# Mixture-of-experts kernel: the second products of a group pair in two groups of three, and another order of the seven first products

## The chip, the cores and the metric

The kernel runs on one core of one Trainium2 chip. The metric is the device time of one execution in microseconds, the median of several runs.

## What is computed

Three layers follow each other: attention with a global and a local part, a mixture of experts whose gate is made even by eight Sinkhorn rounds, and a gated linear layer. The change lies in the second one:

```python
def _moe_ref(x, w_gate, w1, w2):
    N, D = x.shape                      # 1536, 512
    E = w_gate.shape[1]                 # 8
    ...
    for e in range(E):
        h = np.maximum(x @ w1[e], 0.0)  # w1[e]: 512 x 1024
        ye = h @ w2[e]                  # w2[e]: 1024 x 512
        out += P[:, e:e + 1] * ye
    return out.astype(np.float32)
```

All values are float32. The kernel keeps each operand of a matmul as a high part (float32r) and a low part, the remainder, and makes a product from three matmuls: high x high, high x low, low x high (`product`, lines 362 to 370). The lines 368, 369 and 370 are these three, wherever the product comes from.

## The kernel before

Expert 0 is done first, in plain products, while attention and the gate are being computed. Experts 1 to 7 follow in 28 *visits*, seven experts by four quarters of w1's columns (256 columns and the matching 256 rows of w2). Each visit is done by `run_fast` and consists of two *pairs*, one for each half of the batch; a pair is two groups of 384 tokens. There are thus 56 pairs. After them the gated layer runs.

In a pair (`pair`, from line 506) the hidden values x w1 of both token groups, for 2 x 128 columns, are computed with seven block products instead of eight, from sums of blocks of w1 and sums of blocks of x. The seven are the calls `run(0, ...)` to `run(6, ...)`, here R0 to R6. Each is six matmuls with 384 columns of tokens. Three of them read sums of x's blocks, which were formed once and stand in `th` and `tl`; four read blocks of x itself, in `xh` and `xl`. The w1 side is one of seven *forms*, high and low, which `form_step` makes for the next visit: ACT rounds (line 201), POOL takes the remainder (line 202).

The seven results are put together in three PSUM banks x, y and z. A run with `start=False` adds to what stands in its bank. Before it may do so, the earlier content has to be taken: by ACT's copy into `snap` (`copied`, line 560), or by DVE's sum of the bank and a copy (`summed`, line 556), which is followed by ACT's rectified high part (`hidden`, line 546) and DVE's low part (line 548). The low part is put off: it is queued in `late` and issued by `rest()`.

Second products belong to the pair before: six units stand in `pending`, three with the hidden values t, three with o. A unit (`unit_second`), here S, is six matmuls with 512 columns of w2 into one of four banks. Then DVE multiplies the bank by the gate and adds it to the accumulator (line 451); this is called the take-off below. `seconds(count)` issues that many units, and after each one it issues all that is in `late` and calls `slots(None)`.

The order is written out by hand, and each engine works through its own queue in that order:

```python
run(0, x, block(0, 0)); copied(0, x); slots(0)
run(1, z, trans(0)); copied(1, z); slots(1)
seconds(1)
run(2, x, trans(1), start=False); copied(2, x); slots(2)
seconds(1)
run(3, z, block(1, 1), start=False); summed(t_hid, 0, z, snap[:, 2]); slots(3)
seconds(1)
run(4, x, trans(2), start=False); summed(t_hid, 1, x, snap[:, 1]); slots(4)
seconds(1)
run(5, y, block(1, 0)); summed(o_hid, 0, y, snap[:, 0]); slots(5)
seconds(2)
run(6, x, block(0, 1), start=False); hidden(o_hid, 1, x); slots(6)
```

`slots` is called 13 times a pair, seven times after a run and six times after an S. Each call is a *tick*. In the first pair of a visit the ticks after an S issue POOL's four additions of w1's blocks for the next visit (`sum_steps`, line 273). In the second pair the ticks after a run issue the next visit's forms, from the one after R1 on, and the first two ticks after an S issue the splits of the two halves of w2 (128 x 512 each). The seventh form follows the second pair.

Every tick also drives `doubles`. The gated layer's weights come as doubles, and are turned into float32 in 36 pieces in the `work` tile, spread over the ticks of the first 26 visits: 12 steps a piece, 440 steps with eight empty ones over 676 ticks. Six of the twelve issue an operation on DVE (lines 315, 322, 328, 335, 340, 345); the first of these is a shift that ACT converts (line 318) in the same step, two also end in one on POOL (348, 351), one loads and one stores.

Of the kernel before, what the change touches and what calls it, by code (L numbers as in the profile page):

```python
# [66 lines left out]
def tile_global_local_attention__then__sinkhorn_moe__then__glu(  # L67
# [132 lines left out]
    def split_one(r, h, lo):  # L200
        nc.scalar.activation(out=h, in_=r, func=AF.Copy)  # L201
        nc.gpsimd.tensor_tensor(out=lo, in0=r, in1=h.bitcast(F32), op=ALU.subtract)  # L202
# [47 lines left out]
    def form(i):  # L250
        a, col = (1, i) if i < 4 else (0, i - 4)
        cols = slice(col * FQ, (col + 1) * FQ)
        return wh[a][0][:, cols], wl[a][0][:, cols]

    def w1_blocks(n):
        r = raw[visits[n]["raw"]][:, 0 : 4 * FQ]
        r = r.rearrange("p (k f c) -> p f k c", k=KD, f=2)
        return {(i, j): r[:, i, 2 * j : 2 * j + 2, :] for i in range(2) for j in range(2)}

    def tall(ap):  # L260
        return ap.rearrange("p (k c) -> p k c", k=2)

    def sums():
        return [tall(state["sums"][:, i * FQ : (i + 1) * FQ]) for i in range(4)]
# [11 lines left out]

    def form_step(n, i):
        a, (s1, s2, s3, s4) = w1_blocks(n), sums()
        src = (a[0, 0], s1, s2, s4, s3, a[0, 1], a[1, 1])[i]
        h, lo = form(i)  # L280
        split_one(src, tall(h), tall(lo))

# [79 lines left out]
    def product(ps, pairs, start=True):  # L362

        n = len(pairs)
        for i, (ah, al, bh, bl) in enumerate(pairs):
            first, end = start and i == 0, i == n - 1
            mm = dict(out=ps, skip_group_check=not start)
            nc.tensor.matmul(lhsT=ah, rhs=bh, start=first, stop=False, **mm)  # L368
            nc.tensor.matmul(lhsT=ah, rhs=bl, start=False, stop=False, **mm)  # L369
            nc.tensor.matmul(lhsT=al, rhs=bh, start=False, stop=end, **mm)  # L370
# [22 lines left out]
    def next_hid():  # L393
        state["hid"] += 1
        return (state["hid"] - 1) % HID
# [38 lines left out]
    def unit_second(n, t, at, j):  # L434
        vis = visits[n]
        ps = state["Y"].next()
        second(vis, hid[at], j, ps)
        a = acc(t)
        if vis["kind"] != "glu":
            if vis.get("start"):  # L440
                nc.vector.tensor_copy(out=a, in_=ps)
            elif vis["e"] == 0:
                nc.vector.tensor_tensor(out=a, in0=ps, in1=a, op=ALU.add)
            else:
                gate = state["gate"]
                e = vis["e"]
                if e == 1 and vis["f"] == 0:
                    nc.vector.tensor_scalar(
                        out=a, in0=a, scalar1=gate[:, t, 0:1], scalar2=None, op0=ALU.mult
                    )  # L450
                nc.vector.scalar_tensor_tensor(  # L451
                    out=a, in0=ps, scalar=gate[:, t, e : e + 1], in1=a,
                    op0=ALU.mult, op1=ALU.add,
                )
        elif vis["f"] == 0:
            nc.vector.tensor_copy(out=a, in_=ps)
        elif vis["f"] < NFF - 1:
            nc.vector.tensor_tensor(out=a, in0=ps, in1=a, op=ALU.add)
        else:
            o = state["o"].next()  # L460
            nc.vector.tensor_tensor(out=o, in0=ps, in1=a, op=ALU.add)
            nc.sync.dma_start(out=out[t * P : (t + 1) * P, :], in_=o)
# [38 lines left out]
    def tokens(k, s, b, half):  # L501

        at = b * S + half * C
        return xh[:, 2 * k + s, at : at + C], xl[:, 2 * k + s, at : at + C]

    def pair(n, b, slots):


        th, tl = state["t"]
        snap, pre = state["snap"], state["pre"]  # L510
        x, y, z = state["X"].next()[:, :C], state["P2"][:, :C], state["P5"][:, :C]
        t_hid, late = next_hid(), []
        pending, done = state["pending"], []

        def run(i, ps, rhs, start=True):
            h, lo = form(i)
            product(
                ps,
                [
                    (h[:, s * P : (s + 1) * P], lo[:, s * P : (s + 1) * P], *rhs(s))  # L520
                    for s in range(2)
                ],
                start,
            )

        def trans(i):
            return lambda s: (th[:, i, s, b, :], tl[:, i, s, b, :])

        def block(k, half):
            return lambda s: tokens(k, s, b, half)  # L530

        def rest():
            for step in late:
                step()
            late.clear()

        def seconds(count):
            for _ in range(count):
                if pending:
                    unit_second(*pending.pop(0))  # L540
                rest()
                slots(None)

        def hidden(at, f, src):
            hh, hl = hid[at]
            nc.scalar.activation(out=hh[:, f, :C], in_=src, func=AF.Relu)  # L546
            late.append(
                lambda: nc.vector.scalar_tensor_tensor(  # L548
                    out=hl[:, f, :C], in0=src, scalar=0.0, in1=hh[:, f, :C].bitcast(F32),
                    op0=ALU.max, op1=ALU.subtract,  # L550
                )
            )

        def summed(at, f, ps, kept):
            p = pre.next()
            nc.vector.tensor_tensor(out=p, in0=ps, in1=kept, op=ALU.add)  # L556
            hidden(at, f, p)

        def copied(i, ps):
            nc.scalar.activation(out=snap[:, i], in_=ps, func=AF.Copy)  # L560

        run(0, x, block(0, 0))
        copied(0, x)
        slots(0)
        run(1, z, trans(0))
        copied(1, z)
        slots(1)
        seconds(1)
        run(2, x, trans(1), start=False)
        copied(2, x)  # L570
        slots(2)
        seconds(1)
        run(3, z, block(1, 1), start=False)
        summed(t_hid, 0, z, snap[:, 2])
        slots(3)
        seconds(1)
        run(4, x, trans(2), start=False)
        summed(t_hid, 1, x, snap[:, 1])
        slots(4)
        seconds(1)  # L580
        run(5, y, block(1, 0))
        o_hid = next_hid()
        summed(o_hid, 0, y, snap[:, 0])
        slots(5)
        seconds(2)
        run(6, x, block(0, 1), start=False)
        hidden(o_hid, 1, x)
        slots(6)
        for unit in pending:
            unit_second(*unit)  # L590
        rest()
        base = b * TB
        state["pending"] = [(n, base + TC + j, t_hid, j) for j in range(TC)]
        state["pending"] += [(n, base + j, o_hid, j) for j in range(TC)]
# [496 lines left out]
    late = ctx.enter_context(tc.tile_pool(name="late", bufs=1))  # L1091
# [27 lines left out]
    def trans_steps(b):  # L1119


        r21, r11, r12, r22 = (
            work[:, i * 2 * C : (i + 1) * 2 * C].rearrange("p (s c) -> p s c", s=2)
            for i in range(4)
        )

        def block(k, half):
            at = b * S + half * C
            part = slice(2 * k, 2 * k + 2), slice(at, at + C)
            return xh[:, part[0], part[1]], xl[:, part[0], part[1]]  # L1130

        def whole(out, k, half):
            h, lo = block(k, half)
            return lambda: nc.gpsimd.tensor_tensor(
                out=out, in0=h.bitcast(F32), in1=lo.bitcast(F32), op=ALU.add
            )

        def less(out, x, y):
            return lambda: nc.vector.tensor_tensor(out=out, in0=x, in1=y, op=ALU.subtract)

        def put(r, h, lo):
            return lambda: split_one(r, h, lo)

        return [
            whole(r11, 0, 0), whole(r12, 0, 1), whole(r22, 1, 1), whole(r21, 1, 0),
            less(r11, r12, r11), put(r11, th[:, 0, :, b, :], tl[:, 0, :, b, :]),
            less(r12, r22, r12), put(r12, th[:, 2, :, b, :], tl[:, 2, :, b, :]),
            less(r22, r22, r11), put(r22, th[:, 1, :, b, :], tl[:, 1, :, b, :]),
            less(r21, r21, r22), put(r21, *block(0, 1)),
        ]  # L1150
# [94 lines left out]
    trans = [trans_steps(b) for b in range(B)]  # L1245
    side = Paced(gate_steps(), 5 * (NB0 - NA) + 5 * CB * NQ - 4)
    rest = NB0 - NA - 1
# [118 lines left out]
```

## Time and profile before

| | |
|---|---|
| median of 3 runs | 1448.43 us (1444.64 to 1449.32) |
| profiled execution, time | 1444.89 us |
| profiled execution, span of its instructions | 1442.4 us |
| PE busy | 1424.5 us, 99% |
| DVE / ACT / POOL busy | 862.6 / 505.3 / 567.9 us |
| chain that ended last | PE 95%, DVE 2%, ACT 1%, POOL 1%, issue 1% |
| first and last matmul on `th` | 259.2 and 1123.4 us |

The profile lists TensorE twice: PE is the matmuls, PEld the weight loads, which run beside the matmul before. A busy PE only means that a matmul was under way; the pace is read from the distance between the starts of two matmuls. A wait before a matmul sits on its weight load.

### The profile page before, as it was taken

To read this page: it belongs to the slowest core of one execution; us is meant where nothing else is said; L and a number is where in the kernel's file an instruction comes from. 1 tells how busy PE (TensorE), PEld (TensorE's weight loads), DVE (VectorE), ACT (ScalarE), POOL (GpSimd) and SP (SyncE) were. 2 spreads that over 40 slices of the span, in tenths; PEclk is the share of its full clock that TensorE was granted. 3 is DMA by queue.
4 is the path that set the end of the run, shared out by engine and by line. 5 is a ranking of instruction groups with operands and counts; after the bars stand their busy time and mean duration, and the time that the engine had idled before them with its cause. 6 is when DMAs were issued, how large, how long until landed. Compare 5 with 4: busy or idle time off the path is not lost.

```text
span 1442.4 us, 19809 instructions
## 1 busy us (share of the span) xinstructions
PE 1424.5 (99%) x7286; PEld 1229.5 (85%) x7287; DVE 862.6 (60%) x1655; ACT 505.3 (35%) x1152; POOL 567.9 (39%) x618
## 2 busy tenths in 40 slices
PE   8999999999999999999999999999999999999998
PEld 4666888999999999899899999999989888888887
DVE  6676476676657666666676676766665543333333
ACT  5777222433333333333333333333333321222111
POOL 4554454554354453444444444445442221112110
PEclk9999999999999999999999999999999999999999
DMA  7751011132121222221213212212210110010002
GB/s 180 165 141 45 16 45 59 45 103 73 52 74 52 73 73 82 73 69 57 73 52 102 74 52 74 74 52 80 82 51 30 44 45 15 30 44 30 0 1 88
DMA packets 99192, 92.60 MB, mean 64 GB/s; under 512 B 55312, under 2 KB 73744, under 8 KB 99088
## 3 DMA queue, kind: packets, MB, share of 16 engines
q1 hardware_dynamic: 98800, 91.26, 20.4%
q8 instruction: 59, 0.97, 0.3%
q14 instruction: 45, 0.37, 0.1%
q10 hardware_dynamic: 288, 0.00, 0.0%
HBM read 78.66 MB, written 12.58 MB: 63 GB/s over the span
## 4 chain that ended last, share of the span: by engine, by line
PE 95%; DVE 2%; ACT 1%; POOL 1%; issue 1%; DMA 0%; DVEq 0%; ACTq 0%; SPq 0%; POOLq 0%
PE bank L368 30%; PE bank L370 30%; PE bank L369 30%; PE bank L867 1%; PE bank L919 1%; PE bank L905 1%; PE bank L841 1%; ACT e L881 0%; DVE e L875 0%; POOL wl L202 0%; PE bank L1314 0%; POOL e L893 0%; DMA lens<-in_n_local_dram 0%; DMA qr<-in_q_dram 0%; DVE kT L845 0%
## 5 line engine op out<-in xcount | busy, mean ns | idle before, releaser
L451 DVE SCALAR_TENSOR_TENSOR acc<-bank,gate,acc 128x512 f32<-128x512 f32 x336 | 251.7, 749 | 233.8 <-PE bank L370 231.5
L370 PE MATMUL bank<-wh,hl 128*128 128x512 f32 x912 | 358.6, 393 | 0.0
L202 POOL TENSOR_TENSOR wl<-raw,wh 128x512 fp32r<-128x512 f32 (+1 forms) x196 | 209.6, 1086 | 377.4 <-ACT wh L201 377.3
L368 PE MATMUL bank<-wh,hh 128*128 128x512 f32 x912 | 358.1, 393 | 0.0
L369 PE MATMUL bank<-wl,hh 128*128 128x512 f32 x912 | 356.9, 391 | 0.0
L368 PE MATMUL bank<-xh,wh 128*128 128x384 f32 (+1 forms) x720 | 252.8, 351 | 1.1 <-ACT aT L906 1.1
L370 PE MATMUL bank<-xh,wl 128*128 128x384 f32 (+1 forms) x720 | 251.0, 349 | 0.0
L369 PE MATMUL bank<-xl,wh 128*128 128x384 f32 (+1 forms) x720 | 250.0, 347 | 0.0
L370 PEld LDWEIGHTS bank<-wh,hl 128*128 128x128 f32 x912 | 171.0, 188 | 37.6
L546 ACT ACTIVATE hh<-kept 128x384 fp32r<-128x384 f32 x168 | 88.1, 525 | 312.1 <-DVE kept L556 312.1
L368 PEld LDWEIGHTS bank<-wh,hh 128*128 128x128 f32 x912 | 171.4, 188 | 27.1 <-issue 1.3
L369 PEld LDWEIGHTS bank<-wl,hh 128*128 128x128 f32 x912 | 171.3, 188 | 26.2
L368 PEld LDWEIGHTS bank<-xh,wh 128*128 128x128 f32 x720 | 135.2, 188 | 15.0 <-ACT aT L906 1.3
L369 PEld LDWEIGHTS bank<-xl,wh 128*128 128x128 f32 x720 | 135.2, 188 | 13.5 <-DVE xl L1319 0.5
L370 PEld LDWEIGHTS bank<-xh,wl 128*128 128x128 f32 x720 | 135.0, 188 | 5.7
L202 POOL TENSOR_TENSOR wl<-work,wh 128x256 fp32r<-128x256 f32 x112 | 93.8, 839 | 99.4 <-ACT wh L201 96.4
L560 ACT ACTIVATE kept<-bank 128x384 f32<-128x384 f32 x168 | 82.4, 491 | 120.0 <-PE bank L370 119.9
L548 DVE SCALAR_TENSOR_TENSOR hl<-kept,hh 128x384 fp32r<-128x384 f32 x168 | 112.4, 669 | 1.3 <-ACT hh L546 1.3
L370 PE MATMUL bank<-th,wl 128*128 128x384 f32 x336 | 113.0, 336 | 0.0
L368 PE MATMUL bank<-th,wh 128*128 128x384 f32 x336 | 112.4, 334 | 0.0
L369 PE MATMUL bank<-tl,wh 128*128 128x384 f32 x336 | 112.4, 334 | 0.0
L426 DVE TENSOR_TENSOR z<-bank,sg 128x512 f32<-128x512 f32 x36 | 24.9, 692 | 136.2 <-PE bank L370 136.2
(143 smaller groups left out, 1855.3 us busy)
## 6 DMA issues: line engine op xcount, KB each, us to landing
raw<-in_moe_w_dram SPq DMA_DIRECT2D x72, 512.0 KB, 4.3
glw<-work SPq DMA_DIRECT2D x36, 256.0 KB, 2.3
raw<-glw SPq DMA_DIRECT2D x18, 512.0 KB, 3.2
work<-in_moe_w_gate_dram SPq DMA_DIRECT2D x12, 512.0 KB, 3.9
work<-in_moe_w_val_dram SPq DMA_DIRECT2D x12, 512.0 KB, 4.0
work<-in_moe_w_out_dram SPq DMA_DIRECT2D x12, 512.0 KB, 3.9
qr<-in_q_dram SPq DMA_DIRECT2D x32, 96.0 KB, 2.7
kr<-in_k_dram SPq DMA_DIRECT2D x32, 96.0 KB, 2.8
```

The source lines that it names most:

```text
L202: nc.gpsimd.tensor_tensor(out=lo, in0=r, in1=h.bitcast(F32), op=ALU.subtract)
L368: nc.tensor.matmul(lhsT=ah, rhs=bh, start=first, stop=False, **mm)
L369: nc.tensor.matmul(lhsT=ah, rhs=bl, start=False, stop=False, **mm)
L370: nc.tensor.matmul(lhsT=al, rhs=bh, start=False, stop=end, **mm)
L426: nc.vector.tensor_tensor(out=z, in0=ps, in1=sg, op=ALU.mult)
L451: nc.vector.scalar_tensor_tensor(out=a, in0=ps, scalar=gate[:, t, e : e + 1], in1=a, op0=ALU.mult, op1=ALU.add,)
L546: nc.scalar.activation(out=hh[:, f, :C], in_=src, func=AF.Relu)
L548: lambda: nc.vector.scalar_tensor_tensor(out=hl[:, f, :C], in0=src, scalar=0.0, in1=hh[:, f, :C].bitcast(F32), op0=ALU.max, op1=ALU.subtract,)
L560: nc.scalar.activation(out=snap[:, i], in_=ps, func=AF.Copy)
L841: nc.tensor.transpose(ps[:, j * P : (j + 1) * P], raw_[u % QKB][:, j, :], ident)
L867: nc.tensor.matmul(out=ps[j][:, lo:KW], lhsT=qT[rows, own], rhs=kT[rows, keys], start=True, stop=True,)
L905: nc.tensor.transpose(ps[:, j, a, :], e[:, j, a * P : (a + 1) * P], ident)
```

## The change

R0 and R1 change places, and so do R2 and R3, each with its bank, and with them the forms 0 and 1, and 2 and 3. The second products stand in two groups of three: after R3 and after R6, instead of singly after R1, R2, R3 and R4 and in two after R5. The first product behind each group (R4, and R0 of the next pair) reads a sum of x's blocks. `rest` can issue a number of the put-off low parts, and one is issued behind R5 and one behind R6, ahead of the tick.

```diff
--- before.py
+++ after.py
@@ -276,7 +276,7 @@
 
     def form_step(n, i):
         a, (s1, s2, s3, s4) = w1_blocks(n), sums()
-        src = (a[0, 0], s1, s2, s4, s3, a[0, 1], a[1, 1])[i]
+        src = (s1, a[0, 0], s4, s2, s3, a[0, 1], a[1, 1])[i]
         h, lo = form(i)
         split_one(src, tall(h), tall(lo))
 
@@ -529,10 +531,10 @@
         def block(k, half):
             return lambda s: tokens(k, s, b, half)
 
-        def rest():
-            for step in late:
+        def rest(count=None):
+            for step in late[:count]:
                 step()
-            late.clear()
+            del late[:count]
 
         def seconds(count):
             for _ in range(count):
@@ -559,33 +561,32 @@
         def copied(i, ps):
             nc.scalar.activation(out=snap[:, i], in_=ps, func=AF.Copy)
 
-        run(0, x, block(0, 0))
+        run(0, z, trans(0))
+        copied(1, z)
+        slots(0)
+        run(1, x, block(0, 0))
         copied(0, x)
-        slots(0)
-        run(1, z, trans(0))
-        copied(1, z)
         slots(1)
-        seconds(1)
-        run(2, x, trans(1), start=False)
+        run(2, z, block(1, 1), start=False)
+        slots(2)
+        run(3, x, trans(1), start=False)
         copied(2, x)
-        slots(2)
-        seconds(1)
-        run(3, z, block(1, 1), start=False)
         summed(t_hid, 0, z, snap[:, 2])
         slots(3)
-        seconds(1)
+        seconds(3)
         run(4, x, trans(2), start=False)
         summed(t_hid, 1, x, snap[:, 1])
         slots(4)
-        seconds(1)
         run(5, y, block(1, 0))
         o_hid = next_hid()
         summed(o_hid, 0, y, snap[:, 0])
+        rest(1)
         slots(5)
-        seconds(2)
         run(6, x, block(0, 1), start=False)
         hidden(o_hid, 1, x)
+        rest(1)
         slots(6)
+        seconds(3)
         for unit in pending:
             unit_second(*unit)
         rest()
```

The line numbers of the changed kernel are higher by one up to two: `summed` is at 558, `copied` at 562, `hidden` at 548 and 550. Two places of the order, by engine, follow.

DVE in the second pair of a visit, from the first take-off of a second product issued behind R3 to the sums of R4 (`kept<-bank_64`) and R5. `acc<-bank` is a take-off, `hl<-kept,hh` a low part, `work<-work` a step of the doubling. Before:

```order
L451 SCALAR_TENSOR_TENSOR acc_75<-bank_68,gate,acc_75 128x512
L548 SCALAR_TENSOR_TENSOR hl_77<-kept,hh_76 128x384
L328 SCALAR_TENSOR_TENSOR work<-work 128x512
L556 TENSOR_TENSOR kept<-bank_64,kept 128x384
L451 SCALAR_TENSOR_TENSOR acc_75<-bank_69,gate,acc_75 128x512
L548 SCALAR_TENSOR_TENSOR hl_77<-kept,hh_76 128x384
L335 TENSOR_SCALAR work<-work 128x512
L556 TENSOR_TENSOR kept<-bank_65,kept 128x384
```

In the changed kernel:

```order
L451 SCALAR_TENSOR_TENSOR acc_75<-bank_70,gate,acc_75 128x512
L550 SCALAR_TENSOR_TENSOR hl_77<-kept,hh_76 128x384
L451 SCALAR_TENSOR_TENSOR acc_75<-bank_67,gate,acc_75 128x512
L322 TENSOR_SCALAR work<-work 128x512
L451 SCALAR_TENSOR_TENSOR acc_75<-bank_68,gate,acc_75 128x512
L328 SCALAR_TENSOR_TENSOR work<-work 128x512
L558 TENSOR_TENSOR kept<-bank_64,kept 128x384
L558 TENSOR_TENSOR kept<-bank_65,kept 128x384
```

R4's sum stood behind one take-off, one low part and one step of the doubling; now three take-offs, one low part and two steps stand ahead of it, the last step directly ahead. The sum behind it (`kept<-bank_65`, of R5) follows at once.

ACT at the end of a visit, from the high part of R6 (`hh<-bank`) to the copies of the next pair (`kept<-bank`); line 318 is the doubling's conversion, `wh<-raw` a form. Before:

```order
L546 ACTIVATE hh_76<-bank_64 128x384
L318 ACTIVATE work<-work 128x512
L201 ACTIVATE wh_78<-raw_87 128x256 x2
L560 ACTIVATE kept<-bank_63 128x384
L560 ACTIVATE kept<-bank_66 128x384
L560 ACTIVATE kept<-bank_63 128x384
```

In the changed kernel:

```order
L548 ACTIVATE hh_76<-bank_64 128x384
L201 ACTIVATE wh_78<-raw_87 128x256
L318 ACTIVATE work<-work 128x512
L201 ACTIVATE wh_78<-raw_87 128x256
L562 ACTIVATE kept<-bank_66 128x384
L562 ACTIVATE kept<-bank_63 128x384 x2
```

The conversion stands ahead of the next pair's first copy in both, with a form between. The first copy was of bank x (`bank_63`) and is now of bank z (`bank_66`).

## Rows read from the trace of the kernel before

**Rows 1.** The page, parts 1 and 2: busy time by engine, and the granted TensorE clock in 40 slices.

```profile
PE 1424.5 (99%) x7286; PEld 1229.5 (85%) x7287; DVE 862.6 (60%) x1655; ACT 505.3 (35%) x1152; POOL 567.9 (39%) x618
...
PEclk9999999999999999999999999999999999999999
```

**Rows 2.** The view by windows, the seven-product stage: window, its us, busy us (count) of PE, PEld, DVE, ACT, POOL, then clock, DMA share, GB/s.

```profile
258.00:1126.00 868.00, 868.00 (x4333) 783.49 (x4332) 580.34 (x948) 303.51 (x672) 393.65 (x430) 1.00 0.20 67
```

**Rows 3.** The timeline of PE, one pair: start us, us, then line, operation, tiles; first matmuls of blocks.

```profile
801.59 0.33 PE L368 MATMUL bank<-xh,wh 128*128 128x384 f32 x1
...
802.63 0.33 PE L368 MATMUL bank<-th,wh 128*128 128x384 f32 x1
...
807.46 0.34 PE L368 MATMUL bank<-xh,wh 128*128 128x384 f32 x1
...
808.53 0.39 PE L368 MATMUL bank<-wh,hh 128*128 128x512 f32 x1
...
809.92 0.34 PE L368 MATMUL bank<-th,wh 128*128 128x384 f32 x1
...
810.96 0.39 PE L368 MATMUL bank<-wh,hh 128*128 128x512 f32 x1
...
816.17 0.33 PE L368 MATMUL bank<-xh,wh 128*128 128x384 f32 x1
...
817.24 0.33 PE L368 MATMUL bank<-xh,wh 128*128 128x384 f32 x1
```

**Rows 4.** The timeline of PE, second products among second products.

```profile
256.76 0.39 PE L368 MATMUL bank<-wh,hh 128*128 128x512 f32 x1
...
258.12 0.33 PE L368 MATMUL bank<-xh,wh 128*128 128x384 f32 x1
```

**Rows 5.** The timeline of ACT, the copy after R0 of the same pair.

```profile
802.89 0.49 ACT L560 ACTIVATE kept<-bank 128x384 f32<-128x384 f32 x1 [0.55 <-PE bank L370]
```

**Rows 6.** The timeline of DVE, an operation for which a weight load waited.

```profile
186.66 1.00 DVE L1209 TENSOR_TENSOR gate<-gate,rsum 128x96 f32<-128x96 f32 x1
```

**Rows 7.** The timeline of PEld, that weight load.

```profile
187.72 0.30 PEld L1215 LDWEIGHTS bank<-gate,ones 128*128 128x128 f32 x2 [1.96 <-DVE gate L1209]
```

**Rows 8.** The timeline of DVE, the same pair.

```profile
807.66 0.75 DVE L451 SCALAR_TENSOR_TENSOR acc<-bank,gate,acc 128x512 f32<-128x512 f32 x1 [1.67 <-PE bank L370]
808.80 0.56 DVE L556 TENSOR_TENSOR kept<-bank,kept 128x384 f32<-128x384 f32 x1 [0.39 <-PE bank L370]
809.28 0.42 DVE L315 TENSOR_SCALAR work<-work 128x512 int32<-128x512 int32 x1
...
816.14 0.97 DVE L335 TENSOR_SCALAR work<-work 128x512 int32<-128x512 int32 x1
```

**Rows 9.** Groups of DVE by form, 340 to 1110 us: form xcount | busy us, mean ns | idle before.

```profile
L548 DVE SCALAR_TENSOR_TENSOR hl<-kept,hh 128x384 fp32r<-128x384 f32 x148 | 98.4, 665 | 0.0
...
L328 DVE SCALAR_TENSOR_TENSOR work<-work 128x512 int32<-128x512 int32 x33 | 28.5, 863 | 0.1
...
L322 DVE TENSOR_SCALAR work<-work 128x512 int32<-128x512 int32 x33 | 19.3, 586 | 0.0
L315 DVE TENSOR_SCALAR work<-work 128x512 int32<-128x512 int32 x33 | 16.9, 512 | 6.2 <-DMA work<-in_moe_w_gate_dram 5.0 <-DMA work<-in_moe_w_out_dram 1.0 <-DMA work<-in_moe_w_val_dram 0.2
```

**Rows 10.** The view of line 451 (the take-off): min/median/max ns, first and last start.

```profile
L451 DVE SCALAR_TENSOR_TENSOR acc<-bank,gate,acc x336: 734/751/754, 273.3 to 1140.4; 128x512 f32<-128x512 f32 x168
```

**Rows 11.** The view of line 548, the low halves read from SBUF.

```profile
L548 DVE SCALAR_TENSOR_TENSOR hl<-kept,hh x168: 541/551/1549, 267.3 to 1128.7; 128x384 fp32r<-128x384 f32 x168
```

**Rows 12.** The timeline of POOL, the same pair and the next.

```profile
815.99 0.84 POOL L202 TENSOR_TENSOR wl<-work,wh 128x256 fp32r<-128x256 f32 x1 [2.49 <-ACT wh L201]
...
822.32 0.74 POOL L273 TENSOR_TENSOR work<-raw 128x256 f32<-128x256 f32 x1
```

**Rows 13.** Groups of POOL by form, 340 to 1110 us.

```profile
L202 POOL TENSOR_TENSOR wl<-raw,wh 128x512 fp32r<-128x512 f32 x48 | 63.4, 1321 | 6.3 <-ACT wh L201 6.3
```

**Rows 14.** Groups of ACT by form, 340 to 1110 us.

```profile
L318 ACT ACTIVATE work<-work 128x512 f32<-128x512 int32 x33 | 22.1, 669 | 37.1 <-DVE work L315 37.1
```

## The prediction

> **What bounds the kernel now.** I read the busy shares first: PE is busy 99% of the span at a granted clock of 9 tenths or more in every slice, which is the 2.4 GHz level [rows 1]. The change lies in the seven-product visits, so the next view is that stage alone: from 258 to 1126 us PE is busy 868.00 of 868.00 us, DVE 580 and POOL 394 [rows 2]. PE waits for nobody there. Only two things can then change the time: the pace at which PE runs its matmuls, and a wait that PE does not have now.
>
> The pace is read from the starts of six-matmul blocks in one pair of groups [rows 3]. I call the seven runs R0 to R6 by their number in the code, and a second product S. A pair takes from 801.59 to 817.24, 15.65 us, and there are 56 pairs. A block on x after another block on x takes 1.04 us (801.59 to 802.63), a block on a sum of x's blocks right after an S also 1.04 (809.92 to 810.96), but a block on x right after an S takes 1.07 (807.46 to 808.53, and 816.17 to 817.24), and the S that follows a block on x takes 1.39 (808.53 to 809.92). An S among S's takes 1.36 [rows 4].
>
> **The change part by part.** *Pace.* Without any turn a pair would last 7 x 1.04 + 6 x 1.36 = 15.44 us; today's turns cost 0.21. After the change no block on x follows an S (R0 and R4, on sums, do), which takes away three times 0.03. S begins twice a pair instead of five times: once after a block on a sum, once after one on x, where the first S costs 0.03 more and the next some 0.01. I put what is left at 0.05, a pair at 15.49, the gain at 0.16 x 56 = 9.0 us. One turn is new, from a sum to x, twice a pair (R0 to R1, R4 to R5). Nothing in the trace has it; the nearest row is the turn from x to a sum at 802.63, which costs nothing, and the worst is 0.03 as after an S: 2 x 0.03 x 56 = 3.4 less. So between 5.6 and 9.0; I take **8 us gained**, nearer the nearest row.
>
> *The waits that move closer.* R2 adds to the bank that R0 wrote, so it must wait for ACT's copy of it; R3 likewise for the copy after R1; R6 adds to the bank whose sum DVE has to read after R4. Today an S or more lies between: R4 ends at 810.96 and R6 starts at 816.17, 5.2 us [rows 3]. Afterwards one block of 1.04 us lies between in all three places. Is that enough? ACT starts its copy 0.26 us after the block's end (802.63 to 802.89) and takes 0.49 [rows 5], so it is done at 0.75. Where a weight load did wait, it started 0.05 to 0.06 us after DVE's end (187.66 to 187.72) [rows 6, 7]. A load runs one matmul, 0.17 us, ahead of its product, so R2's is due at 1.04 - 0.17 = 0.87, and released at 0.80. DVE's sum starts 0.27 after its block and takes 0.56: released at 0.88, about when due [rows 8]. With ACT and DVE idle beforehand all three just fit. The price is in what stands ahead of them on their queues.
>
> *R6 and DVE.* DVE now has to take off three S's before R4's sum, and the steps that double the last layer's weights are threaded in: each S has a tick, and a step stands directly between the third take-off and R4's sum in 18 of the 56 pairs (counted in the new order; two steps a pair are the rule there). I lay out such a pair, as in the order shown, zero at R3's end, with mean durations [rows 9] and 0.08 of overlap between neighbours on DVE (809.28 starts before 808.80 + 0.56 is over). R2's sum and a shift are done by 1.6. S1 ends at 1.37, its take-off (0.75) runs from 1.6 to 2.35, the low half of t's hidden values (0.67) to 2.94, S2's take-off to 3.61, a step of 0.59 to 4.11. S3 ends at 4.09; a take-off starts 0.20 after (807.46 to 807.66) [rows 8], so 4.29 to 5.04; a step of 0.86 to 5.82; the sum to 6.30, released at 6.35. R6's load is due at 4.09 + 2.08 - 0.17 = 6.00. So 0.35 us late on mean durations; without a step behind the third take-off the sum begins when R4 allows and nothing is late.
>
> The means hide POOL. The low-half step takes 551 ns in the median and 1549 at the most, while the take-off, which reads a PSUM bank, stays within 734 to 754 [rows 10, 11]. At 816.14 a step of the 0.42 kind took 0.97, beginning while POOL ran from 815.99 to 816.83 [rows 8, 12]: DVE's operations without a PSUM operand wait for POOL's, and POOL's for theirs. In the second pair of a visit POOL splits the next visit's weights, the two halves of w2 in 1.32 us each [rows 13]; with the splits of the forms around them they now come tick after tick behind ACT's rounding, just when DVE works off three S's. There each of the three SBUF-only operations meets a POOL operation under way and waits for half of it, about 0.6 instead of the 0.11 to 0.17 in the means (0.665 - 0.551; 0.586 - 0.42): 0.35 + 3 x 0.45 = 1.7; some of them pass free, so I take 1.1. In the first pair POOL only adds weight blocks, which wait for nothing of that pair and run in its first microseconds (822.32 in one that began at 817.24) [rows 3, 12]; there I take 0.2. Of the 18, 10 are second pairs: 10 x 1.1 + 8 x 0.2 = 12.6, say **13 us lost**. Ends: 18 x 0.1 = 2, if POOL's operations always fall beside these, and 18 x 1.7 = 31.
>
> [...]
>
> *R2 and ACT.* A doubling's conversion on ACT (0.67) waits for DVE's shift (0.51) [rows 9, 14]. Where it falls into the pair's last tick, it stands ahead of R0's copy, and the shift behind the last S's take-off: with zero at that S's end, take-off 0.20 to 0.95, shift to 1.4, conversion to 2.1, copy to 2.5, release 2.55, R2's load due at 2.08 - 0.17 = 1.91. That is 0.65 late. 36 conversions over 13 ticks a pair make 3 such pairs: **2 us lost**; none to 4 is possible. Today R2's copy has an S more, and the same conversion hides.
>
> *Free.* The reordered forms on ACT and POOL cost nothing: a form is made a pair ahead of its use. The second products themselves are as many and go to four banks in turn as before.
>
> **The sum**: -8 + 13 + 2 = +7 us. The profiled execution took 1444.89 us (span 1442.4) and would take about 1452; the median of the runs is 1448.43, 3.5 above it, so I forecast **1456** for a median. About 0.3%, 4.3 us, is what a measurement of this kernel can tell from no change.
>
> **The rivals.** *Faster (0.10).* DVE keeps up: the splits fall beside the steps, R6 loses 2 and R2 2, pace gains 8: -4 to -6, about 1443. For it speaks that DVE is busy only two thirds of the stage [rows 2]; against it that a pair with two steps is late even on means. It decides when a pair with a step loses under 0.1 us. *Balance (0.13).* The average loss is some 0.3 us instead of 0.7: 18 x 0.3 + 2 - 8, about zero, 1448. *Every pair waits (0.09).* The three fits of 0 to 0.07 us fail by 0.1 each: 56 x 0.3 = 17 more, about 1470; release rows of only 0.05 us speak against it. *The turn cost stays*, moved from S-to-x to sum-to-x: it is the 3.4 us in the bounds above. A drop of the granted clock behind a wait I leave without a price: a weight load waited 1.96 us at 187.72 [rows 7] in a slice that still shows 9 tenths [rows 1].
>
> **How the numbers follow.** The forecast has 0.68 and reaches from 1453 to 1468; with the case in which every pair waits, slower by over 0.3% has 0.77; balance is 0.13 for within 0.3%, the faster case 0.10. The range 1445 to 1470 leaves out the faster case and the end of the dearest one.
>
> **What would show it.** In the stage's PE idle time there should appear waits of L368 on DVE's sum, in some 15 to 20 pairs, 0.1 to 2 us each, most in second pairs, and about 3 on ACT's copy; outside them a pair should last 15.5 us, and a block on x 1.04. The sum before R6 should start late behind a doubling step, whose duration is stretched by POOL. No PE idle time at all, or pairs without doubling that wait, would make the forecast wrong.

## The result, and the profile after

The changed kernel took 1453.37 us (median of 5 runs, 1453.04 to 1454.49). The kernel before took 1447.01 beside it (1444.64 to 1449.32). The ratio is 1.0051, with a 95% interval of 1.0038 to 1.0065: slower by half a per cent, 6.4 us. The profiled execution took 1454.48 us, with a span of 1452.7.

The times scatter partly because the visits start at another moment in each execution: at 258.12 us in the profile of before, and at 262.27 in that of the same order without doubling (first experiment), which took 3.5 us longer with a stage of the same length. So I compare the stage: from the first matmul of the first R0 to the first transpose of the gated layer. It lasts 873.44 us before (258.12 to 1131.56) and 882.31 after (259.45 to 1141.76). That is 8.9 us more. What follows it lasts 310.9 us in both.

The page of the changed kernel, parts 1 and 2, answers to [rows 1]:

```profile
PE 1424.0 (98%) x7286; PEld 1227.9 (85%) x7287; DVE 873.5 (60%) x1655; ACT 502.2 (35%) x1152; POOL 579.5 (40%) x618
...
PEclk9999999999999999999999999999999999999999
```

It looks unchanged: the granted clock is 9 tenths in every slice and PE's share has only gone from 99% to 98%. The stage by windows (columns as in [rows 2]) tells more. Where PE was busy all 868 us, it is now idle for 9.8 us of 879.

```profile
258.00:1137.00 879.00, 869.20 (x4344) 782.93 (x4343) 593.00 (x951) 302.85 (x678) 407.08 (x432) 1.00 0.20 66
```

PE's waits in the view of waits (line waited for, us in total, times, longest) say whom it waits for. Both lines were absent before:

```profile
PE bank L368 <- DVE kept L558: 8.7, 12, 1.8
...
PE bank L368 <- ACT kept L562: 1.1, 3, 0.5
```

**The pace.** PE's timeline over a pair in which nothing waits, with the starts of R4, R0, R1, R2, R3, the first S of a group and the next R4, answers to [rows 3]:

```profile
566.20 0.34 PE L368 MATMUL bank<-th,wh 128*128 128x384 f32 x1
...
573.45 0.34 PE L368 MATMUL bank<-th,wh 128*128 128x384 f32 x1
...
574.50 0.34 PE L368 MATMUL bank<-xh,wh 128*128 128x384 f32 x1
...
575.55 0.33 PE L368 MATMUL bank<-xh,wh 128*128 128x384 f32 x1
...
576.59 0.33 PE L368 MATMUL bank<-th,wh 128*128 128x384 f32 x1
...
577.62 0.39 PE L368 MATMUL bank<-wh,hh 128*128 128x512 f32 x1
...
581.71 0.34 PE L368 MATMUL bank<-th,wh 128*128 128x384 f32 x1
```

The pair takes 581.71 - 566.20 = 15.51 us, where it took 15.65. Blocks take 1.03 to 1.05 us wherever they stand. The turn from a sum to x, which no row of before showed, costs 0.01 us at most: R0 takes 1.05 us up to R1's start, and so does R1, on x, up to R2's, also on x.

**R6 and DVE.** A second pair of a visit. PE first, up to R6's first matmul:

```profile
535.83 0.34 PE L370 MATMUL bank<-xh,wl 128*128 128x384 f32 x1
537.13 0.44 PE L368 MATMUL bank<-xh,wh 128*128 128x384 f32 x1 [0.97 <-DVE kept L558]
537.41 0.34 PE L369 MATMUL bank<-xl,wh 128*128 128x384 f32 x1
```

R6 was due 0.17 after 535.83 and began 1.13 us late (the row's 0.97 counts from the end of the matmul before, which overlaps the next). DVE's queue ahead of it:

```profile
532.34 0.92 DVE L550 SCALAR_TENSOR_TENSOR hl<-kept,hh 128x384 fp32r<-128x384 f32 x1
533.18 1.51 DVE L335 TENSOR_SCALAR work<-work 128x512 int32<-128x512 int32 x1
534.62 1.40 DVE L451 SCALAR_TENSOR_TENSOR acc<-bank,gate,acc 128x512 f32<-128x512 f32 x2
535.93 0.68 DVE L340 SCALAR_TENSOR_TENSOR work<-work 128x512 f32<-128x512 f32 x1
536.53 0.55 DVE L558 TENSOR_TENSOR kept<-bank,kept 128x384 f32<-128x384 f32 x1
```

POOL in the same stretch:

```profile
532.10 0.74 POOL L202 TENSOR_TENSOR wl<-work,wh 128x256 fp32r<-128x256 f32 x1 [1.79 <-ACT wh L201]
532.80 3.05 POOL L202 TENSOR_TENSOR wl<-raw,wh 128x512 fp32r<-128x512 f32 x2
```

The two halves of w2 are split on POOL from 532.80 to 535.85. Beside POOL's work the low part (line 550) takes 0.92 us where its median is 0.55, and the doubling's step L335 takes 1.51 where its shortest is 0.41. The two take-offs, which read PSUM, take 1.40 together, as they do without POOL beside them (second experiment). Then one more step, L340, stands directly ahead of R4's sum, which ends at 537.08. R6's matmul begins 0.05 later. In this pair each link is the one that the prediction laid out.

**R2 and ACT.** The end of a visit, in the timelines of DVE, ACT and PE:

```profile
417.18 0.42 DVE L315 TENSOR_SCALAR work<-work 128x512 int32<-128x512 int32 x1
```

```profile
417.63 0.69 ACT L318 ACTIVATE work<-work 128x512 f32<-128x512 int32 x1 [4.12 <-DVE work L315]
...
418.52 0.84 ACT L562 ACTIVATE kept<-bank 128x384 f32<-128x384 f32 x2
```

```profile
418.23 0.34 PE L370 MATMUL bank<-xh,wl 128*128 128x384 f32 x1
419.03 0.45 PE L368 MATMUL bank<-xh,wh 128*128 128x384 f32 x1 [0.47 <-ACT kept L562]
```

The shift (L315) comes behind the last take-off, ACT's conversion (L318) behind the shift, a form and the copy behind the conversion. R2's first matmul was due at 418.40 and comes at 419.03, 0.63 late. There are three such places (418.2, 685.9 and 954.2 us): 0.63, 0.33 and 0.63.

**A fall of the clock.** The longest wait, in the first visit, was followed by something that no step of the prediction had. PE's timeline there, and the window that shows the clock:

```profile
281.03 0.34 PE L370 MATMUL bank<-xh,wl 128*128 128x384 f32 x1
283.20 0.44 PE L368 MATMUL bank<-xh,wh 128*128 128x384 f32 x1 [1.84 <-DVE kept L558]
...
283.83 0.52 PE L368 MATMUL bank<-xh,wh 128*128 128x384 f32 x1
284.15 0.53 PE L369 MATMUL bank<-xl,wh 128*128 128x384 f32 x1
...
287.30 0.39 PE L368 MATMUL bank<-wh,hh 128*128 128x512 f32 x1
```

```profile
283.20:287.20 4.00, 4.00 (x12) 3.53 (x13) 3.88 (x5) 2.64 (x7) 3.73 (x5) 0.58 0.00 0
```

After an idle time of 1.84 us, three matmuls run at the usual pace. The next nine take 0.32 us from start to start with 384 columns and 0.43 with 512 (the last 0.38), instead of 0.17 and 0.23. The mean granted clock of these 4 us is 0.58; the slow matmuls go at the 1.2 GHz level. At 287.30 the clock is back. This cost 1.6 us. Two of the five executions, the profiled one among them, have a mean granted clock of 0.997 (1454.48 and 1454.49 us), the other three of 0.999 (1453.04 to 1453.37); only the profiled one has a trace, so it is not known whether the others had this fall.

**The stage's account.** Pace: -7.4 (from the first experiment). Twelve late R6: +10.7 in start times (2.00 and 0.91 in the first visit and at the start of the second; 0.38 to 1.15 in ten second pairs, 7.75 together). Three late R2: +1.6. Each matmul that waited is followed by the next 0.28 us later instead of 0.17 (537.13 to 537.41): 15 x 0.11 = +1.6. The clock: +1.6. That makes +8.1 of the 8.9; the rest lies in starts that are late by 0.11 us or less each.

### The profile page after: what moved, and what is told of

It reads as the page before. It is cut to its first block, busy times and chain, and to the rows that moved or that the text cites. A ratio compares the mean times of both kernels' runs of the same rounds, so it can differ in the third digit from the quotient of the medians.

```text
span 1452.7 us, 19692 instructions
## 1 busy us (share of the span) xinstructions
PE 1424.0 (98%) x7286; PEld 1227.9 (85%) x7287; DVE 873.5 (60%) x1655; ACT 502.2 (35%) x1152; POOL 579.5 (40%) x618
## 4 chain that ended last, share of the span: by engine, by line
PE 89%; DVE 6%; ACT 1%; issue 1%; POOL 1%; DMA 1%; DVEq 0%; ACTq 0%; POOLq 0%; SPq 0%
PE bank L368 28%; PE bank L370 28%; PE bank L369 28%; PE bank L868 1%; DVE acc L451 1%; PE bank L920 1%; PE bank L906 1%; PE bank L842 1%; DVE kept L558 1%; POOL wl L202 1%; ACT e L882 0%; DVE e L876 0%; DVE hl L550 0%; DVE work L328 0%; DVE work L340 0%
## 5 line engine op out<-in xcount | busy, mean ns | idle before, releaser
L202 POOL TENSOR_TENSOR wl<-raw,wh 128x512 fp32r<-128x512 f32 (+1 forms) x196 | 214.7, 1108 | 191.4 <-ACT wh L201 191.1
L558 DVE TENSOR_TENSOR kept<-bank,kept 128x384 f32<-128x384 f32 x168 | 92.7, 555 | 207.8 <-ACT kept L562 181.5
L202 POOL TENSOR_TENSOR wl<-work,wh 128x256 fp32r<-128x256 f32 x112 | 99.7, 896 | 232.8 <-ACT wh L201 229.4
L550 DVE SCALAR_TENSOR_TENSOR hl<-kept,hh 128x384 fp32r<-128x384 f32 x168 | 122.6, 738 | 4.7 <-ACT hh L548 3.8
L348 POOL TENSOR_TENSOR work<-work 128x512 f32<-128x512 f32 x36 | 38.2, 1060 | 190.1 <-DVE work L345 132.8
```

The lines of the kernel that those rows point to most:

```text
L348: nc.gpsimd.tensor_tensor(out=mask, in0=low, in1=high, op=ALU.mult)
L550: lambda: nc.vector.scalar_tensor_tensor(out=hl[:, f, :C], in0=src, scalar=0.0, in1=hh[:, f, :C].bitcast(F32), op0=ALU.max, op1=ALU.subtract,)
```

## The experiments

My theory was that of the prediction: the pace is gained in every pair, and is lost again where steps of the doubling, stretched by POOL's splits, stand ahead of R4's sum, and in a few places ahead of R0's copy. The rivals: the new order is too tight in itself, so that pairs without doubling wait too; or POOL alone makes the loss, and the steps are harmless without it. Eight kernels were run, four at a time, each beside the kernel before (median 1445.87 us beside the first four, 1445.46 beside the others).

| run | median us (range) | ratio to before (95%) | stage us |
|---|---|---|---|
| before | see above | 1 | 873.44 |
| after | 1453.37 (1453.04 to 1454.49) | 1.0051 (1.0038 to 1.0065) | 882.31 |
| no doubling, after | 1438.62 (1438.38 to 1440.7) | 0.9951 (0.9934 to 0.9967) | 867.97 |
| no doubling, before | 1444.71 (1443.76 to 1448.74) | 0.9993 (0.9984 to 1.0003) | 873.44 |
| w2 splits later | 1453.27 (1452.67 to 1455.63) | 1.0058 (1.0041 to 1.0075) | 882.28 |
| four ticks free of doubling | 1443.35 (1441.96 to 1445.98) | 0.9985 (0.9976 to 0.9995) | 871.05 |
| groups of two, one and three | 1442.78 (1441.9 to 1446.55) | 0.9983 (0.9973 to 0.9993) | 871.41 |
| w2 splits later, fetch earlier | 1447.46 (1445.88 to 1451.57) | 1.0016 (1.0007 to 1.0026) | 876.06 |
| five ticks free, late low half | 1442.81 (1440.67 to 1444.65) | 0.9982 (0.9973 to 0.9991) | 870.80 |
| the same, fetch earlier | 1438.41 (1437.76 to 1440.94) | 0.9955 (0.9941 to 0.9969) | 866.66 |

**1. No doubling, in the changed kernel and in the one before.** The list of steps loses its arithmetic in both; the fetch and the store stay:

```diff
-            fetch, no_tick, no_tick, rest, first_a, first_b, keep, kept, scaled, whole, no_tick,
+            fetch, no_tick, no_tick, no_tick, no_tick, no_tick, no_tick, no_tick, no_tick, no_tick, no_tick,
             store,
```

> The changed kernel without the arithmetic of the doubling (its loads and stores stay; the gated layer's weights are then not the reference's). My theory, that R6 waits because doubling steps stand ahead of DVE's sum and meet POOL, and R2 because of the doubling's conversion: the waits go but for the second pair at most, what is left is the pace, 0.13 us x 56 = 7.4 us gained, about 1440 us. Rival, that three take-offs in a row make DVE late by themselves: waits of some 0.2 us or more stay in most of the 56 pairs, and the time stays above 1446 us.

> The kernel before without the arithmetic of the doubling, as the base of the run above. If the doubling is hidden there, as my theory has it: no wait of PE in the stage and the time of before within 1 us, 1447. If the doubling costs PE something in itself, the time falls by as much as in the run above.

The kernel before does not care: its stage is 873.44 us with the doubling and without it. The changed kernel loses 14.3 us of its stage (882.31 to 867.97) and is then faster than before. The rival that the order is too tight in itself falls: of 56 pairs only one waits by more than half a microsecond, in the first visit. DVE's timeline there:

```profile
279.04 1.52 DVE L448 TENSOR_SCALAR acc<-acc,gate 128x512 f32<-128x512 f32 x1
...
281.34 0.65 DVE L448 TENSOR_SCALAR acc<-acc,gate 128x512 f32<-128x512 f32 x1
```

Line 448 scales expert 0's accumulator by its gate. These operations stand between the take-offs of the first two visits and are stretched beside POOL as the doubling's steps are (1.52 us, where the same line takes 0.48 at 281.01 in the profile of after). Taking off this wait (1.52 us) and 0.41 us of delays of 0.11 or less each leaves 866.04: the pace alone is worth 873.44 - 866.04 = 7.4 us.

**2. The splits of w2 later.** The first two ticks after an S no longer issue them; those behind R6 do:

```diff
+        singles = [0]
...
             elif i is None:
-                if seconds:
+                singles[0] += 1
+                if singles[0] > 3 and seconds:
                     seconds.pop(0)()
```

> The changed kernel with the two splits of w2 moved from the first group of second products to the second one, 2 x 1.32 us of POOL out of the stretch ahead of R4's sum; the doubling steps stay where they are. My theory, DVE's operations on SBUF wait for POOL's: the waits before R6 fall from about 11 us to 4 or 5, most under 0.2 us, about 1445 us. Rival, the doubling steps alone make the queue long: the 12 waits stay as they are and the time is 1453.

In time this was a miss: 1453.27 us, no gain. Yet the place that it aimed at did what the theory says. DVE in the same pair as shown above:

```profile
533.20 0.41 DVE L335 TENSOR_SCALAR work<-work 128x512 int32<-128x512 int32 x1
533.53 1.40 DVE L451 SCALAR_TENSOR_TENSOR acc<-bank,gate,acc 128x512 f32<-128x512 f32 x2
534.86 0.68 DVE L340 SCALAR_TENSOR_TENSOR work<-work 128x512 f32<-128x512 f32 x1
535.45 0.54 DVE L558 TENSOR_TENSOR kept<-bank,kept 128x384 f32<-128x384 f32 x1
```

L335 takes 0.41 us instead of 1.51, all else is equal, and the sum ends at 535.99 instead of 537.08. R6's wait there falls from 1.13 to 0.03 us, and seven such waits fall from 0.51 to 1.15 to at most 0.09. This shows POOL's part. But the first two visits still wait. In the first the wait is 0.97 us instead of 2.00, about as much less as line 448 takes (0.48 instead of 1.51); in the second it is 2.06 instead of 0.91. And three new waits came, of 2.36, 1.44 and 2.57 us (at 393.0, 551.5 and 708.7); around two of these five the clock fell as well (last section). The first of the new ones, in DVE's and PE's timelines, and what led to it on POOL and SP:

```profile
391.27 0.75 DVE L451 SCALAR_TENSOR_TENSOR acc<-bank,gate,acc 128x512 f32<-128x512 f32 x1 [0.61 <-PE bank L370]
394.58 0.43 DVE L315 TENSOR_SCALAR work<-work 128x512 int32<-128x512 int32 x1 [2.56 <-DMA work<-in_moe_w_out_dram]
```

```profile
392.99 0.34 PE L370 MATMUL bank<-xh,wl 128*128 128x384 f32 x1
395.53 0.44 PE L368 MATMUL bank<-xh,wh 128*128 128x384 f32 x1 [2.20 <-DVE kept L558]
```

```profile
383.88 3.24 POOL L202 TENSOR_TENSOR wl<-raw,wh 128x512 fp32r<-128x512 f32 x3
```

```profile
387.14 0.93 SPq L185 DMA_DIRECT2D raw<-in_moe_w_dram  x2
...
388.68 0.38 SPq L311 DMA_DIRECT2D work<-in_moe_w_out_dram  x1
```

The shift L315 that begins a piece waited 2.56 us for its fetch, and R4's sum stands behind it. The fetch was issued at 388.68, behind two loads of 512 KB, and these had waited for the last of POOL's three operations in the row above, which ends at 387.12: the remainder of the seventh form, behind the two splits of w2. The view of DMA issues, for this stretch (last column: us from issue to landing):

```profile
work<-in_moe_w_out_dram SPq DMA_DIRECT2D x1, 512.0 KB, 5.8
```

and for the whole changed kernel, the median of twelve:

```profile
work<-in_moe_w_out_dram SPq DMA_DIRECT2D x12, 512.0 KB, 3.8
```

In the changed kernel the fetch stood behind the same two loads, was issued at 388.66 and landed after 5.5 us. But there R4 came at 393.54 instead of 391.07, and the shift, at 394.41, found its data. I had moved POOL's splits without following the buffers that they free: POOL is done with them later against the visit, the loads into them start later, and the fetch behind these on SP's queue comes too late for a step that stands ahead of R4's sum.

**3. The same, with the fetch earlier.** To test that reading, the fetch got four empty ticks behind it instead of two:

```diff
-            fetch, no_tick, no_tick, rest, first_a, ...
+            fetch, no_tick, no_tick, no_tick, no_tick, rest, first_a, ...
```

> The run with w2's splits moved later, and two more empty steps between a piece's fetch and its first step, some three ticks or 4 us. Theory from the trace of that run: its three long waits (2.4, 1.4 and 2.6 us) come from a shift on DVE whose fetch lands late, behind two loads of the next weights on the same queue; they go, or fall by more than half, and the time falls from 1453 to 1445 to 1447. Rival, the long waits come from the length of DVE's queue: three or more waits over 1 us stay behind the second visit, 1452.

Two of the three new waits (1.44 at 551.5 us, 2.57 at 708.7) are gone, the one at 393 shrank from 2.36 to 1.16 (its shift still waits 1.35 us for its fetch), and the time fell by 5.8 us, to just above the range that I had given. Some 1.6 us of that, by what the fall above cost, is one fall of the clock less. Three small ones are new (0.53, 0.27 and 0.27). The waits of the first two visits (0.97 and 2.35) stay, and two waits on ACT are left. Late fetches made most of the miss; they are not the whole loss.

**4. Four ticks without doubling.** The ticks of the first group of S and the last one of the pair issue no step; the steps go to the other nine:

```diff
+        place = [0]
+
+        def paced():
+            at = place[0] % 13
+            place[0] += 1
+            if at not in (4, 5, 6, 12):
+                side()
...
-            side()
+            paced()
...
-    doubles = Paced([*[no_tick] * 8, *double_steps()], 26 * (last - F0 - 1))
+    doubles = Paced([*[no_tick] * 8, *double_steps()], 18 * (last - F0 - 1))
```

> The changed kernel with the doubling's ticks left out behind R3, behind the three second products of the first group but the one behind R3 kept, and behind the last one of the pair; nine ticks a pair instead of thirteen, all the work stays. (Left out are the fifth, sixth, seventh and thirteenth tick.) My theory: no step between R3's sum and R4's sum, no conversion ahead of R0's copy: the three waits on ACT go, those on DVE fall to 2 or 3 us in two or three pairs, about 1441 us, faster than the kernel before. Rival, that the loss is in the three take-offs or in the banks: the waits stay, above 1450.

The stage is 11.3 us shorter than after's, with POOL's splits where they were: without a step among the three take-offs they do no harm behind the first two visits. With the second experiment this settles the rival on POOL: the regular waits need both, the steps and the splits, and go with either. All three waits on ACT are gone too. Four waits on DVE stay: two in the first two visits (0.93 and 1.21 us), where line 448 stands, and two at 547.5 and 704.4 (1.60 and 0.50); in both a shift had waited for its fetch (2.78 and 1.95 us).

**5. Groups of two, one and three.** The third S of the first group goes behind R4:

```diff
-        seconds(3)
+        seconds(2)
         run(4, x, trans(2), start=False)
         summed(t_hid, 1, x, snap[:, 1])
         slots(4)
+        seconds(1)
```

> The changed kernel with the third second product of the first group put back behind R4, so that 2.4 us instead of 1.04 lie between R4's end and R6; all doubling steps stay. My theory, the loss is the short distance from R4 to R6 with DVE late: the waits on DVE's sum before R6 fall from 10.7 us in 12 pairs to 2 at most, the three on ACT's copy (1.6 us) stay, R5 now follows a second product and a pair costs 0.05 us of pace more; about 1443 to 1445 us. Rival, that the number of turns or the banks set the time: slower than the changed kernel by some 2 us, 1455.

An S between R4 and R6 gives DVE's sum room, and two waits of 0.40 us are all that is left there. The three waits on ACT are untouched (0.64, 0.33 and 0.64), since R0's copy still has one block of cover. The stage without all five waits would be 871.41 - 2.4 - 5 x 0.11 = 868.5, so that some 5 us of the pace remain of 7.4. A third group costs its turns again: a pair in which nothing waits takes 15.55 us here, and 15.51 in the changed kernel.

**6. Five ticks free, and a low half put off.** The kernel of 4, with the tick behind R3 free as well, and the low part of t's first half issued behind R4's sum:

```diff
-            if at not in (4, 5, 6, 12):
+            if at not in (3, 4, 5, 6, 12):
...
-                rest()
+                if len(pending) < 3:
+                    rest()
...
         summed(t_hid, 1, x, snap[:, 1])
+        rest(1)
...
-    doubles = Paced([*[no_tick] * 8, *double_steps()], 18 * (last - F0 - 1))
+    doubles = Paced([*[no_tick] * 8, *double_steps()], 16 * (last - F0 - 1))
```

> A version meant to be faster than both: the changed kernel without doubling ticks behind R3, behind the three second products of the first group and behind the last one of the pair (eight ticks a pair), and with t's first low half put off behind R4's sum, so that only the three take-offs stand ahead of that sum. Theory: waits of PE in two or three pairs, 1 to 3 us in all with what a late fetch adds, pace gain 7.4: 1440 to 1443 us. Rival, that three take-offs are late by themselves: above 1446.

It is no faster than 4: two waits on DVE's sum are left (0.48 and 0.82 us), and a new one of 2.80 on ACT, in the same pair as the 0.82, took what the edit gave. DVE, ACT and PE there:

```profile
699.72 0.43 DVE L315 TENSOR_SCALAR work<-work 128x512 int32<-128x512 int32 x1 [8.57 <-DMA work<-in_moe_w_gate_dram]
```

```profile
700.18 0.65 ACT L318 ACTIVATE work<-work 128x512 f32<-128x512 int32 x1 [7.14 <-DVE work L315]
700.74 0.47 ACT L563 ACTIVATE kept<-bank 128x384 f32<-128x384 f32 x1
```

```profile
698.23 0.39 PE L370 MATMUL bank<-wh,hl 128*128 128x512 f32 x1
701.26 0.45 PE L368 MATMUL bank<-th,wh 128*128 128x384 f32 x1 [2.64 <-ACT kept L563]
```

It is the late fetch again. DVE stood idle for 8.57 us before the shift; the fetch had been issued at 692.92, behind two loads at 691.91, and so 6.8 us before the shift began. ACT's conversion stands behind the shift, and the copy behind the conversion.

**7. The same, with the fetch earlier.** Kernel 6 with the edit of 3:

> The version of the run before with two more empty steps between fetch and shift. Theory: no shift waits for its fetch any more, waits of 1 us at most in all, 1439 to 1441 us. If late fetches play no part with the free ticks, the same time as without the empty steps, within 1 us.

It took 1438.41 us and beats both kernels, the one before by 0.45% (0.31 to 0.59). Its stage by windows:

```profile
258.00:1125.00 867.00, 867.00 (x4359) 784.99 (x4358) 575.66 (x955) 305.33 (x681) 396.32 (x435) 1.00 0.20 68
```

PE is busy all the time again, as in [rows 2], and the stage is 6.8 us shorter than before. Three shifts still wait for their fetch (2.9 us the longest), but PE does not wait for them. It does the whole of the doubling, and yet comes within 0.7 us of the 866.0 that the pace alone gave: the gain of the new order can be had with little lost.

## Why the prediction was right, point by point

The sign, the size (1456 forecast, 1453 measured) and the mechanism held, but the size in good part by luck. The places that the prediction had named make little of the 8.9 us: seven second pairs with a step behind the third take-off lose 6.6 and R2 1.6, which is 9.3 with the 0.11 behind each wait, and the pace gives 7.4 back. That leaves 1.9, by itself hardly to be told from no change. The other 7 came from what it had not named or not priced: the first two visits (2.9), three second pairs without such a step (1.1), the 0.11 behind these five waits (0.5), the clock (1.6) and small delays (0.8). By its steps:

- *Pace, 8 us gained.* 7.4 measured. It lay between the bounds, and the turn from a sum to x costs 0.01 us at most, nearer to the row it was put beside than to the dearest one.
- *R6 and DVE, 13 us lost.* This was right in the whole, less so in its parts. A step directly between the third take-off and R4's sum stands in 18 pairs, 10 of them second pairs, as counted. But the eight first pairs lose under 0.1 us where I took 0.2, and of the ten second pairs eight wait: the first visit's (2.00) and seven more (0.51 to 1.15). In the other two, at 440.8 and 976.8, the splits of w2 began only when the last step did. And three second pairs without a step behind the third take-off wait 0.38 us each, against my sentence that nothing is late there: two steps between the take-offs were stretched. DVE in one of these three, then DVE and POOL in one of the two that did not wait:

```profile
376.13 1.24 DVE L328 SCALAR_TENSOR_TENSOR work<-work 128x512 int32<-128x512 int32 x1
...
377.95 0.86 DVE L335 TENSOR_SCALAR work<-work 128x512 int32<-128x512 int32 x1
```

```profile
441.69 0.42 DVE L322 TENSOR_SCALAR work<-work 128x512 int32<-128x512 int32 x1
```

```profile
441.72 3.26 POOL L202 TENSOR_TENSOR wl<-raw,wh 128x512 fp32r<-128x512 f32 x2 [1.59 <-ACT wh L201]
```

  The layout on mean durations (0.35 late) was too dark: with POOL's splits away, the seven pairs are 0.09 us late at most. The first two visits cost 2.9 us (2.00 and 0.91), where line 448's scalings stand between the take-offs. I had not looked for other operations there; of the 2.00, 1.52 stay without any step. The 0.91 fell in a first pair, where I had POOL's additions of w1's blocks run early: there they came behind two of the doubling's own operations on POOL, and ran beside DVE (a scaling at 297.74 took 0.95 us). With the 0.11 us behind each wait the whole term is 12.0.
- *R2 and ACT, 2 us lost.* 1.6 in three places, as counted, each late by 0.33 or 0.63 against 0.65.
- *POOL and DVE.* The pair with the split taken away shows the price by itself: 1.51 to 0.41 us for one step, and 1.1 us of wait. The Trainium skill (SBUF — State Buffer, Who interferes with whom) has the one that starts first hold the shared ports to its end. The trace agrees: L335 began at 533.18, 0.38 us into the first split of w2, and took 1.1 us more. By the same section of the Trainium skill an operation of VectorE with at most one SBUF input stays clear of this only outside the modes that use both ports, and plain `tensor_scalar` is among those that can enter them. L335 is a `tensor_scalar` with one SBUF input, and in this pair it was stretched most; that it ran in such a mode is not shown by itself.
- *Free.* The reordered forms cost nothing; no wait of the stage is on them.
- *A drop of the clock, left without a price.* This step failed. I argued from one wait of 1.96 us on a weight load in a slice at 9 tenths [rows 7]; here an idle time of 1.84 cost 1.6 us, and the slices of the page still show 9 tenths, because 4 us vanish in a slice of 36.
- *The rivals.* That every pair waits is refuted by the kernel without doubling. That DVE keeps up is what the runs without the doubling and with five free ticks and the earlier fetch reach: it was the right case for a kernel with less ahead of the sum and the copy.

Three things stay open. The waits of the first two visits have several causes (scalings, steps, POOL) that were only in part tried apart. The kernels 6 and 7 change ticks and a low half together, so what each gives is not told apart. And the fall of the clock is not explained (below).

## What to carry to other kernels

An order that groups like work together can raise the pace of a saturated engine, but it takes away cover elsewhere: for each consumer whose slack shrinks, list everything that stands ahead of its producer in that engine's queue, with durations taken beside the engine that shares its ports, not their means. Background work that is dealt out by ticks should then be kept out of the few ticks ahead of that producer; that gave more here than moving the other engine's work. When any of it is moved, follow the buffers that it frees: the loads that wait for these can hold up a fetch behind them on the same queue, and a step that waits for that fetch stops the whole queue.

## What the runs showed of the hardware that I had not expected

- The granted clock can fall after a short wait of PE. It did at waits of 2.00 us (after, 0.58 over 283.2 to 287.2), of 2.06 and 2.57 (splits later) and of 2.35 (splits later, fetch earlier), and did not at 1.52 (no doubling), 2.36 (splits later, at 393) and 2.80 (five ticks free). The length of the wait alone does not decide it. The window after the longest of these:

```profile
701.20:705.20 4.00, 3.28 (x17) 2.96 (x18) 3.96 (x8) 1.06 (x3) 0.00 (x0) 1.00 0.00 0
```

- A matmul that waited is followed by the next after 0.28 us instead of 0.17 (283.20 and 537.13 above), so a wait costs 0.11 us more than its length.
- A fetch of 512 KB that was issued 1.5 us behind two loads of that size landed 5.5 to 5.8 us after its issue, where the median of twelve is 3.8.
